# Windowed attention and a gated feed-forward on one core: the raw keys of unit 3 move from the opening's list of steps to the head of the next list, and that list's order changes

## The chip, the cores and the metric

The kernel runs on one core of a Trainium2 chip. The metric is the device time of one execution in microseconds (us); lower is better. The engines are TensorE (PE in the profile, with its weight loads as PEld), VectorE (DVE), ScalarE (ACT), GpSimd (POOL) and SyncE (SP). SP computes nothing; it only issues transfers between DRAM and the chip's memory.

## The reference

Attention over 4 batches, 8 heads, 768 tokens of 64 numbers, then a feed-forward of 512 to 2048 to 512 over the 3072 tokens. Each query sees the keys less than 16 positions away, and 24 more keys and values that are the maximum and the mean of each block of 32 tokens:

```python
k_sum = k.reshape(B, H, nb, block, D).max(axis=3)
v_sum = v.reshape(B, H, nb, block, D).mean(axis=3)
scores_l = scale * np.matmul(q, k.transpose(0, 1, 3, 2))
mask_l = np.abs(pos[:, None] - pos[None, :]) < window
scores_s = scale * np.einsum('bhsd,bhnd->bhsn', q, k_sum) + np.log(block)
...
a = np.exp(scores_all - np.max(scores_all, axis=-1, keepdims=True))
a = a / (np.sum(a, axis=-1, keepdims=True) + 1e-09)
attn = np.matmul(a, np.concatenate([v, v_sum], axis=2))
...
h = x @ w_in
g = np.where(h >= 1, h, np.where(h <= -1, 0.0, (h + 1) ** 2 / 4))
out = g @ w_out
```

All of it is float32.

## The kernel before

**Units.** The tokens are worked in seven units, numbered 0 to 6 in the code: four of 384 tokens and three of 512. "Unit 3" of the title is the third, index 2 in the code, and its steps have a 2 as their first digit; below, units go by the index. Each unit has an attention part, in four pairs of heads (p = 0 to 3), and a feed-forward part, in sixteen blocks of 128 hidden columns (f = 0 to f in hexadecimal). While the feed-forward of unit c runs, the attention of unit c+1 is worked beside it. A float32 product is made of three products of high and low halves, so each weight block is once split into halves: a weight is fetched raw, ACT scales its top words (L237) and its low words (L243), DVE joins them (L250, L255), ACT, DVE or POOL takes the high half (L265) and POOL the rest (L269). This conversion goes on beside units 0 and 1. Units 4 to 6 work with "sets": sums and differences of weight blocks that are kept in DRAM during units 1 to 3 (L636 to L643) and loaded again into the places of the weight blocks by POOL (L580).

**Order.** The whole work is two strings of steps, OPENING and REST. A program walks through each string and issues each step's instructions at once, and each engine runs what it was given strictly in that order; a wait at the head of an engine's queue holds up everything behind it. SP's queue holds all loads and stores but those of the sets, which stand in POOL's queue between its computing. Between the two strings, POOL clears two buffers (L754, L757) that take over memory of the opening.

**Steps.** A step is a letter and hexadecimal digits, mostly unit, pair or block, and part. `r20` is `load_raw_keys(2, 0)`: one DMA of 384 KB (L292). `R20` is `sum_keys`: DVE's maximum over blocks of 32 keys (L352). `C200` is `summary_keys`: POOL copies these maxima into the key tile (L357), beside the window keys that `k20` loads (L303). `s20` multiplies that key tile with the queries of `q20` on PE (L510). `v13` is `load_vals(1, 3)` (L337), `A13` the product that reads those values (o_ps, L449). `y20` loads raw values (L324) and `u20` sums them on DVE (L367). `wf` fetches the last pair of weight blocks to be converted, raw (its two DMAs are `raw<-in_w_out` of L228), `af` is ACT's first pass over it (L237), `bf0`, `bf1` the second (L243), `cf0` to `cf3` the joins on DVE (L250, L255). F is the first product of the feed-forward (`h`, L571), G, H, I, J, O its gate (ACT L664, ACT L668, DVE L672, ACT L677, POOL L682), B the second product (`acc`, L695). T transposes scores (t_ps, L437), N gives their norms (POOL L432), X and L split attention outputs (L460, L465). `{460` loads part 0 of set 6 (L580), and `1460` is the first product that reads it (L594).

**Buffers.** The tiles of the raw keys of units from 2 on, of the raw values of these units and of the windowed values of unit 1 share one tag with two buffers:

```python
def load_raw_keys(c, p):
    k_raw = input_tile(stage, "kraw", [P, S], c, p) if c < 2 else load.tile([P, S], F32, tag="v", name=f"kraw{c}_{p}", bufs=2)
    nc.sync.dma_start(out=k_raw, in_=kT[BEGINS[c][0], p])
...
        v_ts[c, p] = input_tile(load, "v", [P, NB, P], c, p)
```

A DMA into a buffer waits on SP's queue until the last reader of the tile before it is done.

Of the kernel before, what the change touches and what calls it, by code (L numbers as in the profile page):

```python
# [10 lines left out]
I32 = mybir.dt.int32  # L11
U32 = mybir.dt.uint32
# [49 lines left out]
c83 F081 I06 F082 F083 bb1 J07 r20 bb0 F0a0 O07 v11 J06 F0a1 ab q13 F0a2 F0a3 c82 E110 cb0 O06 cb2 cb1 d8 E111 e8 cb3  # L62
D111 G08 B06 N111 H08 db I08 aa S12 W10 M121 ba1 M120 J08 ba0 G0a we f121 ca1 B07 eb F090 F091 ca0 F092 F093 ca3 H0a
ca2 D110 A10 E121 O08 T111 I0a da ac P111 v13 bc1 B08 G09 X10 cc1 F0c0 ea bc0 H09 cc3 F0c1 ad I09 J09 J0a N110 wf cc0
f120 bd0 F0c2 F0b0 O09 cc2 dc F0b1 bd1 cd0 O0a cd2 C13 F0b2 L10 cd1 F0c3 W11 F0b3 B09 T110 E120 D121 cd3 G0c G0b P110
H0b S13 A11 dd H0c B0a ec M130 I0b q21 ed I0c F0d0 D120 k20 ae F0d1 F0e0 F0e1 J0c F0e2 v12 F0d2 M131 J0b f130 be0 r21
f131 ce0 N120 O0c be1 E130 ce2 O0b af D130 F0d3 X11 N121 R20 ce1 F0e3 ce3 B0b L11 E131 G0d H0d I0d B0c bf1 de ee cf1
bf0 G0e H0e T120 I0e cf0 F0f0 cf3 J0d O0d W13 F0f1 cf2 D131 F0f2 J0e df F0f3 T121 q20 G0f F110 H0f F111 W12 P121 N130
P120 N131 T130 A12 X12 I0f T131 P131 L12 F100 J0f P130 B0d O0e R21 ef O0f A13 X13 F112 L13 C200 F101 F102 F113 F103
B0e G11 G10 H10 H11 I10 B0f J10 I11 F120 J11 O10 F121 F122 O11 F123  # L70
# [3 lines left out]
i20 F141 g203 H13 g200 z20 I13 g202 g205 g204 F142 F143 B10 F160 F161 F162 F163 B11 J12 g201 u21 O12 %012 h20 %013 G16  # L74
l201 l200 H16 o01 &10 o02 z21 B12 %001 %000 J13 O13 G14 I16 t202 t20a %014 t205 y22 r22 F150 H14 t209 %002 t207 t200
t206 F151 v20 &61 B13 C210 %015 I14 t208 F170 F171 F152 J16 %016 J14 x200 %017 F153 %003 t204 t20b t203 t201 %004 O14
O16 G15 p20 H15 X20 &05 q22 %005 R22 %006 L20 u22 I15 B14 &01 s21 J15 F172 %007 n211 v21 n210 y23 &02 r23 F173 G17
%101 F180 F181 i21 H17 I17 &51 &11 &03 %100 k22 q23 &04 F182 %102 g213 %103 z22 g212 g211 g215 g214 g210 F183 O15 %104
G18 h21 H18 F190 I18 %105 u23 l210 l211 F191 x210 t216 F192 t215 F193 B15 t219 t21b t214 t210 t212 t211 t217 F1a0 F1a1
J17 F1a2 B16 F1a3 %106 O17 %107 t213 G19 &12 t218 %110 H19 J18 t21a B17 O18 p21 %111 I19 &13 %112 G1a H1a &50 I1a %113  # L80
F1c0 F1c1 X21 C220 L21 F1c2 %114 s22 %115 F1b0 F1b1 %116 n220 n221 %200 i22 J19 %117 %201 g224 F1b2 g223 g225 g220 B18
O19 F1c3 R23 J1a O1a %202 z23 g222 F1b3 g221 %203 h22 G1c %204 H1c G1b I1c v22 &15 k23 l220 l221 H1b %205 B19 I1b %206
F1d0 x220 %207 J1b F1d1 F1d2 F1d3 F1f0 F1f1 O1b t220 t228 t224 t223 G1d F1f2 &14 H1d t222 t225 t221 t22b t227 B1a %210
C230 t229 t22a %211 t226 p22 J1c X22 I1d F1e0 y40 &20 &23 %212 O1c %213 F1e1 L22 F1e2 %214 %215 s23 %301 n231 n230 i23
F1e3 %216 F1f3 G1e B1b %300 H1e g234 g231 v23 &22 g233 J1d I1e %302 F200 %217 g232 %303 &24 k30 g230 O1d %304 g235
F201 G1f H1f %305 x230 F202 h23 B1c %306 J1e &25 &31 l231 l230 I1f %307 O1e t233 t235 t230 t234 F210 %311 q30 %310
F211 &33 B1d J1f B1e t23a t23b t232 t236 t239 t238 t231 O1f t237 p23 X23 u40 %312 %313 L23 B1f F203 C300 U10 G20 s30
F212 %314 H20 %315 o10 %316 n301 F213 G21 I20 J20 n300 H21 F230 F231 F232 i30 g302 g301 I21 %317 r40 k31 v30 &35 J21
g300 U11 g303 g305 g304 O20 F233 F220 G23 F221 F222 F223 O21 G22 H23 B20 o11 h30 l301 l300 x300 C310 H22 I23 %401 I22
# [732 lines left out]
```

## Time and profile before

| what | value |
| --- | --- |
| time, median of 3 runs | 630.86 us (630.76 to 632.21) |
| the profiled execution's own time | 630.26 us |
| its span (first to last instruction) | 628.5 us |
| TensorE's mean granted clock | 0.989 of full speed |
| PE busy | 609.4 us, 97% of the span |
| PEld, DVE, ACT, POOL busy | 85%, 70%, 58%, 63% |
| transfers | 122.56 MB, 195 GB/s on the mean |

Busy times are sums over the span. A share near 100% says that an engine hardly ever rests; where it does rest is read from stretches of the trace (windows), and why, from what released it (waits).

### The profile page before, as it was taken

Reading aid. Unit: us, or ns where it says so; the run is one execution under the profiler, and the core shown is the slowest. Engines: PE = TensorE matmul, PEld = TensorE weight load, DVE = VectorE, ACT = ScalarE, POOL = GpSimd, SP = SyncE. Lnnn points to the kernel's source line nnn. Section 1 sums busy time; section 2 is a strip of 40 time slices with the busy share of each in tenths; the row PEclk is TensorE's granted clock in tenths of the full one; section 3 lists DMA queues with packets and bytes.
Section 4 is the critical chain, followed back from the end, with each engine's and each line's share of the span. In section 5 each row is a group of like instructions: output and inputs, shape, how many; then the busy total and the mean of one; then the engine's idle time right before and its main releaser. Section 6 shows DMA issues by size and latency. Waiting matters only on the chain.

```text
span 628.5 us, 12987 instructions
## 1 busy us (share of the span) xinstructions
PE 609.4 (97%) x4628; PEld 535.5 (85%) x4628; DVE 437.9 (70%) x1012; ACT 365.0 (58%) x977; POOL 393.7 (63%) x450
## 2 busy tenths in 40 slices
PE   8689998999999999999999999999999999999996
PEld 7578887788888888898888988879988898989895
DVE  5879785568887789778676788865777765444342
ACT  2779997456454655565465665537556365553542
POOL 2578997655676677663477865669674568735421
PEclk9879999999999999999999999999999999999998
DMA  8989835476554667355678497767696485676521
GB/s 305 329 238 382 269 100 142 140 275 202 155 157 159 171 169 216 103 141 133 178 216 270 116 304 231 196 197 217 184 302 175 124 269 146 175 225 186 172 64 67
DMA packets 85041, 122.56 MB, mean 195 GB/s; under 512 B 27377, under 2 KB 56305, under 8 KB 84977
## 3 DMA queue, kind: packets, MB, share of 16 engines
q1 hardware_dynamic: 71152, 77.68, 40.6%
q0 software_dynamic: 13824, 44.05, 23.9%
q8 instruction: 37, 0.61, 0.4%
q14 instruction: 28, 0.22, 0.1%
HBM read 100.73 MB, written 20.97 MB: 194 GB/s over the span
## 4 chain that ended last, share of the span: by engine, by line
PE 89%; DVE 3%; DMA 2%; ACT 2%; POOL 2%; issue 2%; SPq 0%; POOLq 0%; ACTq 0%; DVEq 0%
PE acc L695 41%; PE h L571 20%; PE h L594 19%; PE o_ps L559 3%; PE s_ps L510 3%; DMA halves<-sets 1%; PE o_ps L449 1%; PE t_ps L437 1%; DMA first<-in_kT 1%; PE s_ps L403 1%; ACT raw L237 1%; DVE den L416 1%; PE h_idle L650 0%; DVE vs L361 0%; DVE e L410 0%
## 5 line engine op out<-in xcount | busy, mean ns | idle before, releaser
L695 PE MATMUL acc<-halves,ghi 128*128 128x512 f32 x720 | 224.2, 393 | 0.0
L682 POOL TENSOR_TENSOR glo<-t,ghi 128x384 fp32r<-128x384 f32 (+1 forms) x112 | 126.9, 1135 | 108.6 <-ACT ghi L677 98.9
L695 PEld LDWEIGHTS acc<-halves,ghi 128*128 128x128 f32 x720 | 135.5, 188 | 24.5
L571 PE MATMUL h<-x,halves 128*128 128x384 f32 x720 | 140.5, 342 | 3.1 <-POOL halves L269 2.2
L695 PE MATMUL acc<-halves,glo 128*128 128x512 f32 x360 | 143.0, 397 | 0.0
L594 PEld LDWEIGHTS h<-halves,halves 128*128 128x128 f32 x1008 | 132.4, 190 | 9.6 <-issue 1.8
L664 ACT ACTIVATE t<-h,ones_half 128x256 f32<-128x256 f32 (+1 forms) x160 | 80.2, 513 | 101.0 <-DVE h L607 56.7
L594 PE MATMUL h<-halves,halves 128*128 128x256 f32 x1008 | 135.7, 283 | 1.0 <-DMA halves<-sets 1.0
L571 PEld LDWEIGHTS h<-x,halves 128*128 128x128 f32 x720 | 125.1, 188 | 11.1 <-POOL halves L269 3.1
L672 DVE SCALAR_TENSOR_TENSOR t<-h,t 128x256 f32<-128x256 f32 (+1 forms) x160 | 73.6, 472 | 48.4 <-ACT t L668 44.2
L550 DVE STREAM_TRANSPOSE turned_blocks<-e 32x256 f32<-32x256 f32 (+1 forms) x240 | 98.4, 410 | 5.8 <-POOL e L538 1.8
L677 ACT CAST ghi<-t 128x384 fp32r<-128x384 f32 (+1 forms) x112 | 61.9, 556 | 60.3 <-PE acc L695 38.6
L695 PEld LDWEIGHTS acc<-halves,glo 128*128 128x128 f32 x360 | 67.8, 188 | 12.0 <-issue 1.3
L580 POOL DMA_DIRECT2D halves<-sets x96 | 53.1, 556 | 31.8 <-PE h L594 30.6
L668 ACT ACTIVATE t<-t 128x256 f32<-128x256 f32 (+1 forms) x160 | 71.0, 458 | 2.9
L528 ACT ACTIVATE e<-e,den 128x120 f32<-128x120 f32 x144 | 55.0, 383 | 18.6 <-DVE den L524 18.4
L607 DVE TENSOR_TENSOR sums_so_far<-h,sums_so_far 128x256 f32<-128x256 f32 x72 | 29.5, 421 | 34.2 <-PE h L594 29.0
L607 DVE TENSOR_TENSOR h<-h,sums_so_far 128x256 f32<-128x256 f32 x96 | 39.0, 426 | 20.2 <-PE h L594 18.8
L538 POOL TENSOR_TENSOR e<-e,den 128x480 f32<-128x480 f32 (+1 forms) x40 | 35.6, 910 | 26.3 <-DVE den L533 12.1
L269 POOL TENSOR_TENSOR halves<-w,halves 128x1024 fp32r<-128x1024 f32 x15 | 36.1, 2409 | 5.7 <-DMA q<-in_q 4.2
L517 DVE SCALAR_TENSOR_TENSOR e<-s_ps,mask_sb 128x480 f32<-128x480 f32 (+1 forms) x40 | 22.8, 602 | 14.0 <-PE s_ps L510 14.0
L630 POOL TENSOR_TENSOR merged<-merged,high_of_sums 128x512 fp32r<-128x512 f32 x16 | 20.7, 1296 | 17.8 <-ACT high_of_sums L628 17.6
(115 smaller groups left out, 688.7 us busy)
## 6 DMA issues: line engine op xcount, KB each, us to landing
halves<-sets POOLq DMA_DIRECT2D x72, 512.0 KB, 4.8
raw<-in_w_in SPq DMA_DIRECT2D x15, 512.0 KB, 10.3
raw<-in_w_out SPq DMA_DIRECT2D x15, 512.0 KB, 9.6
v<-in_vwin SPq DMA_DIRECT2D x22, 288.0 KB, 4.0
out<-o SPq DMA_DIRECT2D x24, 256.0 KB, 3.8
halves<-sets POOLq DMA_DIRECT2D x24, 256.0 KB, 4.3
kraw<-in_kT SPq DMA_DIRECT2D x13, 384.0 KB, 4.3
vraw<-in_vT SPq DMA_DIRECT2D x13, 384.0 KB, 4.3
```

The costliest lines, as they stand in the source:

```text
L528: nc.scalar.activation(out=e, in_=e, func=AF.Exp, bias=dens[c, p][:, 0, u:u + 1], scale=1.0, accum_out=dens[c, p][:, 1, u:u + 1])
L550: nc.vector.transpose(out=turned_blocks[kb * SB:(kb + 1) * SB, :2 * nt, qb * SB:(qb + 1) * SB], in_=e[qb * SB:(qb + 1) * SB, :, at:at + SB])
L571: nc.tensor.matmul(hs[c, f][:, :w], weight["win", f][:, part, k * P:(k + 1) * P], x, start=(k == 0 and n == 0), stop=(k == NK - 1 and n == 2))
L580: nc.gpsimd.dma_start(out=at[:, 0] if n == 3 else at.rearrange("p h n -> p (h n)"), in_=cols)
L594: nc.tensor.matmul(hs[c, q, n][:, :HALF], weights[:, wp, kk], x[:, xp, kk], start=(kk == 0 and m == 0), stop=(kk == 1 and m == 2))
L607: nc.vector.tensor_tensor(out=of if to is None else so_far[:, to], in0=of, in1=so_far[:, so], op=ALU.add)
L664: nc.scalar.activation(out=t, in_=h, func=AF.Relu, bias=ones_half, scale=0.5)
L668: nc.scalar.square(out=t, in_=t)
L672: nc.vector.scalar_tensor_tensor(out=t, in0=h, scalar=1.0, in1=t, op0=ALU.max, op1=ALU.min)
L677: nc.scalar.copy(out=hi, in_=ts[c, f])
L682: nc.gpsimd.tensor_tensor(out=lo, in0=ts[c, f], in1=hi.bitcast(F32), op=ALU.subtract)
L695: nc.tensor.matmul(acc[c, i], a[:, rows], weight["wout", f][:, part], start=(f == first and n == 0), stop=(f == last and n == 2))
```

## The change

No step is added or taken away. Five steps (`r20`, `r21`, `R20`, `R21`, `C200`) leave OPENING, whose other steps keep their order, and stand near the head of REST. REST is also put in another order in two long parts: from its beginning to about 435 steps in (feed-forward of unit 1, attention of unit 2), and from about 1075 to 1510 (feed-forward of units 3 and 4, attention of unit 5); behind that, a few neighbours change places. The lines of OPENING that lost a step, and the head of REST:

```diff
-c83 F081 I06 F082 F083 bb1 J07 r20 bb0 F0a0 O07 v11 J06 F0a1 ab q13 F0a2 F0a3 c82 E110 cb0 O06 cb2 cb1 d8 E111 e8 cb3
+c83 F081 I06 F082 F083 bb1 J07 bb0 F0a0 O07 v11 J06 F0a1 ab q13 F0a2 F0a3 c82 E110 cb0 O06 cb2 cb1 d8 E111 e8 cb3 D111
...
-H0b S13 A11 dd H0c B0a ec M130 I0b q21 ed I0c F0d0 D120 k20 ae F0d1 F0e0 F0e1 J0c F0e2 v12 F0d2 M131 J0b f130 be0 r21
-f131 ce0 N120 O0c be1 E130 ce2 O0b af D130 F0d3 X11 N121 R20 ce1 F0e3 ce3 B0b L11 E131 G0d H0d I0d B0c bf1 de ee cf1
+S13 A11 dd H0c B0a ec M130 I0b q21 ed I0c F0d0 D120 k20 ae F0d1 F0e0 F0e1 J0c F0e2 v12 F0d2 M131 J0b f130 be0 f131 ce0
+N120 O0c be1 E130 ce2 O0b af D130 F0d3 X11 N121 ce1 F0e3 ce3 B0b L11 E131 G0d H0d I0d B0c bf1 de ee cf1 bf0 G0e H0e
...
-P120 N131 T130 A12 X12 I0f T131 P131 L12 F100 J0f P130 B0d O0e R21 ef O0f A13 X13 F112 L13 C200 F101 F102 F113 F103
+T130 A12 X12 I0f T131 P131 L12 F100 J0f P130 B0d O0e ef O0f A13 X13 F112 L13 F101 F102 F113 F103 B0e G11 G10 H10 H11
...
-y21 U01 U00 U02 F130 y20 &41 &30 k21 &21 &40 o00 %011 s20 F131 &00 u20 G12 %010 F132 F133 n201 H12 I12 n200 G13 F140
...
+F130 U00 &40 r20 r21 k21 &11 R20 C200 U01 y20 o01 F131 G12 U02 F132 R21 H12 s20 I12 o00 y21 n201 F133 F160 v20 G13
```

**SP's queue in the opening.** The first piece shows SP before, from the raw weights of block pair 12 (`raw_943`) on; a name ends in a running number of its buffer, `kraw_0` is `r20`, `v_1` is `v11`, `v_3` is `v13`, `raw_1178` is `wf`, and `q_1` and `k_0` are `q21` and `k20`.

```order
L228 DMA raw_943<-in_w_out 128x1024
L225 DMA raw_943<-in_w_in 128x4x256
L292 DMA kraw_0_984<-in_kT 128x768
L337 DMA v_1_993<-in_vwin 96x768
L319 DMA q_3_1002<-in_q 64x6x64 x2
L228 DMA raw_wout_1074<-in_w_out 128x1024
L225 DMA raw_win_1075<-in_w_in 128x4x256
L337 DMA v_3_1138<-in_vwin 96x768
L228 DMA raw_1178<-in_w_out 128x1024 x2
```

The same place of SP's queue after the change, and on to the place where the raw keys now stand, behind a store of a weight block into the sets (`&40`).

```order
L225 DMA raw_943<-in_w_in 128x4x256
L337 DMA v_1_991<-in_vwin 96x768
L319 DMA q_3_1000<-in_q 64x6x64 x2
L228 DMA raw_wout_1072<-in_w_out 128x1024
L225 DMA raw_win_1073<-in_w_in 128x4x256
L337 DMA v_3_1136<-in_vwin 96x768
L228 DMA raw_1176<-in_w_out 128x1024 x2
L319 DMA q_1_1286<-in_q 64x6x64 x2
L303 DMA k_0_1297<-in_kwin 128x720
L337 DMA v_2_1317<-in_vwin 96x768
L319 DMA q_0_1435<-in_q 64x6x64 x2
L636 DMA sets<-halves_881 128x1024
L292 DMA kraw_0_1602<-in_kT 128x768
```

The load of the raw keys no longer stands ahead of `v11` and takes a buffer of its tag there; what stood behind it moves up one place in the same order, and the two loads of raw keys follow all of the opening's loads.

**POOL's queue where REST begins.** Before, the copy of the key maxima (`C200`, L357) stands ahead of the two gate rows of unit 1 and of the clearing of the two buffers.

```order
L682 TENSOR_TENSOR glo_15_1493<-t_15_1444,ghi_15_1492 128x384
L357 COPY k_0_1299<-ks_0_1356 128x6x24
L682 TENSOR_TENSOR glo_0_1568<-t_0_1553,ghi_0_1567 128x384
L682 TENSOR_TENSOR glo_1_1576<-t_1_1551,ghi_1_1575 128x384
L754 MEMSET turned_blocks 128x1024
L757 MEMSET sums 128x128
L621 TENSOR_TENSOR merged_1_1625<-halves_345 128x256 x2
```

After the change it stands behind them:

```order
L682 TENSOR_TENSOR glo_15_1487<-t_15_1438,ghi_15_1486 128x384
L682 TENSOR_TENSOR glo_0_1559<-t_0_1544,ghi_0_1558 128x384
L682 TENSOR_TENSOR glo_1_1567<-t_1_1542,ghi_1_1566 128x384
L754 MEMSET turned_blocks 128x1024
L757 MEMSET sums 128x128
L357 COPY k_0_1297<-ks_0_1609 128x6x24
L621 TENSOR_TENSOR merged_1_1665<-halves_345 128x256
```

The copy has moved behind four rows of POOL, and on PE `s20`, which reads what it writes, has moved behind two steps of F (`F131`, `F132`).

**POOL's queue at the loads of set 6.** Before: `halves_1020`, `halves_881`, `halves_805` and `halves_941` (DMA rows of L580) are the places that parts 2, 1, 0 and 3 of set 6 go to, `glo_8` is a gate row, and `xraw` and `v_3` are tiles of the attention.

```order
L484 TENSOR_TENSOR xraw_0_4413<-xraw_0_4413 128x512
L379 COPY v_3_4756<-zeros 32x512
L580 DMA halves_1020<-sets 128x1024
L580 DMA halves_881<-sets 128x1024
L580 DMA halves_805<-sets 128x1024
L682 TENSOR_TENSOR glo_8_4970<-t_8_4919,ghi_8_4969 128x512
L580 DMA halves_941<-sets 128x512
```

After, in POOL's order:

```order
L580 DMA halves_941<-sets 128x512
L580 DMA halves_1131<-sets 128x1024
L580 DMA halves_1040<-sets 128x1024
...
L379 COPY v_3_4832<-zeros 32x512
L580 DMA halves_1018<-sets 128x1024
L682 TENSOR_TENSOR glo_8_4974<-t_8_4923,ghi_8_4973 128x512
L580 DMA halves_805<-sets 128x1024
L580 DMA halves_881<-sets 128x1024
```

Part 0 (`halves_805`) has moved ahead of part 1, part 3 (`halves_941`) far ahead of both, and the gate row between part 2 and these.

## Rows read from the trace of the kernel before

**Rows 1.** Windows: us, busy time of each engine (instructions), clock, DMA share, GB/s

```profile
60.00:80.00 20.00, 19.55 (x120) 17.01 (x119) 15.66 (x31) 19.97 (x41) 18.96 (x15) 1.00 0.82 266
80.00:100.00 20.00, 19.98 (x162) 17.41 (x161) 15.98 (x34) 18.51 (x41) 18.51 (x15) 1.00 0.38 111
100.00:120.00 20.00, 16.97 (x127) 14.35 (x127) 11.62 (x24) 11.21 (x28) 14.27 (x16) 1.00 0.40 109
...
400.00:420.00 20.00, 19.04 (x144) 16.61 (x144) 16.40 (x43) 12.25 (x38) 13.27 (x18) 1.00 0.86 240
```

**Rows 2.** PE's timeline: start us, us, instruction, [idle before <-what ended it]

```profile
106.37 0.49 PE L437 MATMUL t_ps<-ident_sb,e 128*120 128x128 f32 x3
108.44 2.34 PE L571 MATMUL h<-x,halves_win 128*128 128x384 f32 x12 [1.58 <-DVE t L672]
111.66 0.55 PE L437 MATMUL t_ps<-ident_sb,e 128*120 128x128 f32 x3 [0.88 <-DVE w L255]
...
113.83 0.54 PE L437 MATMUL t_ps<-ident_sb,e 128*120 128x128 f32 x3 [0.57 <-POOL e L432]
114.30 0.92 PE L449 MATMUL o_ps<-pt,v 120*64 120x64 f32 x24
...
128.65 0.85 PE L510 MATMUL s_ps<-k,q 64*64 64x120 f32 x24
```

**Rows 3.** ACT's timeline

```profile
79.61 1.14 ACT L237 ACTIVATE raw<-raw 128x1024 f32<-128x1024 f32 x1
...
103.96 1.15 ACT L237 ACTIVATE raw<-raw 128x1024 f32<-128x1024 f32 x1 [2.93 <-DMA raw<-in_w_out]
```

**Rows 4.** SP's timeline around the raw keys

```profile
69.35 1.09 SPq L292 DMA_DIRECT2D kraw<-in_kT  x1
85.00 0.33 SPq L337 DMA_DIRECT2D v<-in_vwin  x1
...
96.05 0.33 SPq L337 DMA_DIRECT2D v<-in_vwin  x1
96.83 1.06 SPq L228 DMA_DIRECT2D raw<-in_w_out  x2
```

**Rows 5.** SP's waits, 60 to 130 us: in all, times, longest

```profile
SPq L337 <- PE o_ps L449: 22.6, 2, 14.5
```

**Rows 6.** The page, DMA issues: line, count, KB each, median us to landing

```profile
halves<-sets POOLq DMA_DIRECT2D x72, 512.0 KB, 4.8
...
raw<-in_w_out SPq DMA_DIRECT2D x15, 512.0 KB, 9.6
```

**Rows 7.** DVE's timeline

```profile
101.35 0.92 DVE L352 TENSOR_REDUCE ks<-kraw 128x24 f32<-128x768 f32 x1
...
107.74 0.56 DVE L672 SCALAR_TENSOR_TENSOR t<-h,t 128x384 f32<-128x384 f32 x1 [1.68 <-ACT t L668]
...
110.93 1.28 DVE L255 SCALAR_TENSOR_TENSOR w<-raw,c 128x512 int32<-128x512 int32 x2
...
123.31 1.02 DVE L672 SCALAR_TENSOR_TENSOR t<-h,t 128x384 f32<-128x384 f32 x2 [3.04 <-ACT t L668]
```

**Rows 8.** POOL's timeline

```profile
105.55 1.29 POOL L269 TENSOR_TENSOR halves_win<-w,halves_win 128x512 fp32r<-128x512 f32 x1
...
112.99 1.54 POOL L432 TENSOR_TENSOR e<-e,den 128x360 f32<-128x360 f32 x2
...
128.64 0.20 POOL L757 MEMSET sums<- 128x128 f32 x1
...
404.97 1.05 POOL L580 DMA_DIRECT2D halves<-sets  x2 [2.05 <-PE h L594]
```

**Rows 9.** The chain that ended last, 400 to 416 us: start us, us, what

```profile
405.49 8.45 DMA halves<-sets
```

**Rows 10.** DMA issues, 60 to 85 us: count, KB each, median us to landing

```profile
raw<-in_w_in SPq DMA_DIRECT2D x2, 512.0 KB, 8.2
kraw<-in_kT SPq DMA_DIRECT2D x1, 384.0 KB, 8.1
```

More of the change, by code (lines that the diff above doesn't have):

```diff
@@ new lines @@
+G08 B06 N111 H08 db I08 aa S12 W10 M121 ba1 M120 J08 ba0 G0a we f121 ca1 B07 eb F090 F091 ca0 F092 F093 ca3 H0a ca2
+D110 A10 E121 O08 T111 I0a da ac P111 v13 bc1 B08 G09 X10 cc1 F0c0 ea bc0 H09 cc3 F0c1 ad I09 J09 J0a N110 wf cc0 f120
+bd0 F0c2 F0b0 O09 cc2 dc F0b1 bd1 cd0 O0a cd2 C13 F0b2 L10 cd1 F0c3 W11 F0b3 B09 T110 E120 D121 cd3 G0c G0b P110 H0b
+S13 A11 dd H0c B0a ec M130 I0b q21 ed I0c F0d0 D120 k20 ae F0d1 F0e0 F0e1 J0c F0e2 v12 F0d2 M131 J0b f130 be0 f131 ce0
+N120 O0c be1 E130 ce2 O0b af D130 F0d3 X11 N121 ce1 F0e3 ce3 B0b L11 E131 G0d H0d I0d B0c bf1 de ee cf1 bf0 G0e H0e
@@ L71 @@
+T120 I0e cf0 F0f0 cf3 J0d O0d W13 F0f1 cf2 D131 F0f2 J0e df F0f3 T121 q20 G0f F110 H0f F111 W12 P121 N130 P120 N131
+T130 A12 X12 I0f T131 P131 L12 F100 J0f P130 B0d O0e ef O0f A13 X13 F112 L13 F101 F102 F113 F103 B0e G11 G10 H10 H11
+I10 B0f J10 I11 F120 J11 O10 F121 F122 O11 F123
 """
 REST = """
[L73 to L74 removed]
@@ L75 @@
[L75 to L89, printed above, removed]
@@ new lines @@
+9430 J45 G441 G440 (421 x511 {442 O45 t519 t514 (420 H441 1432 H440 (423 t516 t512 t515 t513 t517 t510 (422 I440 t518
+(453 I441 x520 u53 {440 s52 n521 (450 o32 n520 J44 {443 i52 9431 g527 g520 g521 1436 (452 1434 g525 g524 g522 g523
+g526 z52 p51 1433 9432 X51 9434 1435 O44 {441 {452 x521 9437 9436 G461 G470 1431 h52 9435 H461 G471 H470 (440 l520
+H471 (451 (442 l521 I461 9433 (443 I470 (441 I471 J47 G460 1443 1440 9440 k53 O47 v53 1444 t522 t529 t521 t520 1442
+t52a {463 (470 H460 {450 {451 t525 C530 t524 t526 I460 J46 t527 (472 9441 1441 (471 t528 t52b O46 ^50 {453 1446 9442
@@ new lines @@
+O4a p53 X53 9465 (4b2 1470 <50 G4d1 s60 (4b1 H4d1 (4b3 n600 I4d1 x600 {471 ^51 1465 ^52 >50 n601 9466 1466 (4a2 1461
+9467 {501 {503 G4d0 H4d0 I4d0 9463 {502 (4a0 G4c1 J4d G4c0 9470 i60 1471 {500 <51 (4a3 O4d H4c0 1472 (4a1 H4c1 g601
+g603 I4c0 9473 (4d3 I4c1 (4d2 >51 9471 1474 1473 {510 ^53 9472 9474 (4d0 9475 1475 1476 J4c g605 <52 g600 g604 g607
+g606 <54 O4c G4f1 9476 g602 h60 H4f1 I4f1 G4f0 9477 >52 G4e0 H4f0 G4e1 I4f0 >54 <53 H4e1 <55 l600 l601 >53 (4c2 (4d1
+(4c3 1500 (4c0 1504 I4e1 H4e0 9500 <56 >55 J4f 1502 (4c1 I4e0 9501 1501 1503 t601 9502 O4f {511 J4e t604 1505 1510
@@ new lines @@
+1603 G600 H600 9604 9602 (5e0 (5e2 (5e3 I600 >66 9605 <65 1606 >65 G611 H611 (5e1 9607 I611 U51 G601 U50 H601 1605
+9606 I601 G610 1614 1610 1612 H610 9610 {623 {622 {621 I610 o51 o50 {620 9611 1613 9612 9614 1611 J60 J61 O61 1616
+1615 O60 9617 9615 G631 9613 9616 (611 H631 U52 I631 G630 G621 H630 U53 G620 (613 (603 (601 (612 (602 (610 H621 H620
+{632 {630 I630 I621 J63 I620 1620 (600 9620 J62 O63 1622 1624 O62 1621 (632 (633 (630 9621 9622 9623 1623 1626 (631
+G640 1625 (622 (620 (623 9624 {631 9625 9627 9626 G651 G641 H641 H651 G650 H650 H640 (621 I650 I651 I641 1630 1634
@@ new lines @@
+1660 J6b O68 {673 9660 G6a1 {670 (682 O6b {672 H6a1 (683 G6a0 H6a0 (681 I6a0 I6a1 (680 1664 (6b2 (6b0 1662 (6b1 1663
+9661 9664 J6a 9662 9665 G6d1 (6b3 O6a H6d1 {671 I6d1 (6a3 1665 1666 (6a1 1661 (6a0 9667 9666 9663 G6d0 (6a2 H6d0 I6d0
+G6c1 1670 1674 J6d H6c1 9670 G6c0 I6c1 1672 9671 9672 H6c0 O6d 1673 9674 I6c0 (6d1 1675 9675 (6d3 1676 J6c G6f1 1671
+(6d2 (6d0 O6c 9676 G6f0 H6f1 H6f0 I6f1 9677 9673 G6e1 I6f0 G6e0 J6f H6e0 (6c2 H6e1 O6f (6c0 (6c3 (6c1 (6f0 I6e1 I6e0
+J6e O6e (6f1 (6f3 (6f2 (6e2 (6e0 (6e1 (6e3 U62 U60 U61 U63 o62 o63 o61 o60
```

169 lines of the change are left out of this document (80 added, 89 removed).

## The prediction

> **What bounds the kernel now.** I read the windows first, then PE's timeline where they show a gap, then the timelines of the engines that PE waited for, and last SP's queue. PE is busy for 97% of the span, so the question is only where it is not. In the windows [rows 1] the reader is to compare the first busy column with 20: 19.98 from 80 to 100 us, 16.97 from 100 to 120, 19.04 from 400 to 420. The windows between, and those behind up to 600, show 19.9 or more. Time that is won ahead of such windows is won at the end, since PE's order there doesn't depend on when it starts; so two gaps count, 20 - 16.97 = 3.03 us and 20 - 19.04 = 0.96 us.
>
> PE's timeline [rows 2] splits the first one: 1.58 us before the last half-block of F0f, released by the gate's DVE row of L672; 0.88 us before the next transposes, released by a weight join (L255), which holds the same kind of accumulator; 0.57 us before the third, released by POOL's norms (L432). Together 3.03 us, the whole gap. Three engines are named, but one lateness stands behind them. ACT stood idle for 2.93 us up to 103.96 [rows 3], waiting for the raw weights of the last pair (`wf`). All that ACT does behind it, gate and conversion, is late, and DVE and POOL with it: 107.74, 110.93 and 112.99 [rows 7, 8].
>
> Why were these weights late? SP issued them at 96.83 [rows 4], and they took some 7 us. They stood behind `v13`, and `v13` behind `v11`. SP's waits [rows 5] say that two loads of L337 waited 22.6 us in all for the products that read earlier values, the longest 14.5 us. The timeline shows them [rows 4]: `kraw` (r20) goes out at 69.35 and takes one of the two buffers; `v11` must wait for the other until 85.00, when `A10` has read `v10`; `v13` must wait for `v11` to be read, until 96.05. So raw keys that REST needs sit in a buffer for 32 us (69.35 to their maximum on DVE at 101.35 [rows 7]) and leave one buffer for three values.
>
> **The opening after the change.** `r20` is gone from SP's queue there. `v11` finds a free buffer and goes out at about 69.4; the queries and the weights of block pair 13 follow it as soon as a transfer before them lands. `v13` is now the one that waits for `A10`, so it goes out at 85.0, where `v11` went (PE was full up to there, so `A10` keeps its time). `wf` follows 0.8 us later (96.83 - 96.05 [rows 4]), at 85.8 and 86.4. With the median landing of this load, 9.6 us [rows 6], the second lands at 96.0; ACT is ready for it at 103.96 - 2.93 = 101.03 [rows 3]. That leaves 5 us to spare, so ACT's wait of 2.93 us goes.
>
> What is late next, gap by gap, is found by shifting each row by 2.93 us:
> - Gate row L672 ends at 107.74 + 0.56 - 2.93 = 105.37. PE reaches the place at 108.44 - 1.58 = 106.86. POOL's lower half of the same weights ended at 105.55 + 1.29 = 106.84 [rows 8], and it gets earlier by the 0.92 us of `R20`, which leaves DVE ahead of the join that it waits for [rows 7]: 105.9. The 1.58 us are all won.
> - The first of the two joins ended about 111.57 (half of 1.28 us behind 110.93), so 108.64. PE gets there at 111.66 - 2.46 = 109.20. The 0.88 us are won.
> - The first norm ends at 112.99 + 0.77 - 2.93 = 110.83. PE gets there at 113.83 - 3.03 = 110.80. This one is at its edge; I leave 0.2 us of it, and at most all 0.57 us.
>
> So the opening gives 3.03 - 0.2 = 2.8 us; 1.58 if only the first gap closes.
>
> As to how much a window lost, the Trainium skill (Perfetto Trace Analysis, Identifying the Most-Contended Engine) holds matmul busy time to be a bad measure and the busy share of weight loads a good one. By that the stretch from 100 to 120 us did 14.35 us of loads where its neighbour did 17.41 [rows 1], an estimate of 20 x (1 - 14.35 / 17.41) = 3.5 us lost instead of 3.03. I stay with 3.03, which is the sum of named waits; the two stretches hold different mixes of product lengths.
>
> **The head of REST, where the five steps now stand.** Their work is the same and moves: two loads, 0.92 us twice on DVE, one short copy on POOL. `r20` waits for `A12`, which ends at 114.30 + 0.92 - 2.8 = 112.4 [rows 2]; `r21` for `A13`. The one slow landing that the trace shows took 8.1 us [rows 10], so the keys are there at 120.5. `R20` stands on DVE behind the gate rows that ended at 123.31 + 1.02 = 124.33 [rows 7], now 121.5; before them DVE was idle for 3.04 us, so both sums are hidden. `C200` now stands behind POOL's two clearings, which ended at 128.84 [rows 8], and ends some 0.3 us later, 129.1 less 2.8. `s20` on PE, which reads it, started at 128.65 [rows 2]; two steps of F of 3 products each, 2.34 / 12 = 0.195 us a product, now stand ahead of it, so it comes at 129.8 less 2.8. That is 0.7 us of cover; without it, each late microsecond costs one. I put the edit at 0.
>
> **The loads of set 6.** The gap at 413 us is a wait for one load. The chain [rows 9] shows it issued at 405.49 and landing after 8.45 us, where the median of its kind is 4.8 [rows 6]. It was the second of a pair that POOL issued at 404.97 [rows 8], so one load of 512 KB more stood ahead of it. The new order puts it ahead of that one, and part 3 well ahead of both. At the window's 240 GB/s [rows 1] 512 KB take 2.1 us, more than the wait of 0.96 us, but POOL still waits for the reader of the place, and a gate row stands ahead. I take 0.7 us, with 0 and 0.96 as bounds.
>
> **The rest of the reordering** (units 1 to 4) lies in windows where PE never waits, so it can win nothing; its possible loss is a rival.
>
> **The sum.** 630.26 - 2.8 - 0.7 = 626.8 for the profiled execution. The median stands 0.6 above it (630.86), so 627.4. Ends of this case: 630.86 - 3.03 - 0.96 = 626.9 and 630.86 - 1.58 = 629.3.
>
> **Rivals.**
> 1. *Another engine takes over.* Only the first gap closes, since joins and norms were the true limit of the other two, and the load of set 6 stays as late: 629.3. For it: the third gap has no margin in my own working. Against it: each row behind 103.96 follows ACT. 0.12.
> 2. *The change doesn't do what it says.* `v13` still waits for `A11`, because the buffers come round in another order, and `wf` goes out at 96.8: 630.86 - 0.7 = 630.2. 0.04.
> 3. *The transfers collide.* Without the long wait, `v11`, two query loads and the weights of pair 13 (288 + 192 + 1024 KB) follow at once on those of pair 12, while 60 to 80 us moves 266 GB/s already [rows 1]: 1504 less 384 KB of raw keys is 4.3 us of transfer. If all of that fell on the loads ahead, the last of them, out before 69.35 and there 8.2 us later by its median [rows 10], at 77.5, would land at 81.8, where ACT takes it at 79.61 [rows 3]: 2.2 us late, of which ACT's idle 1.5 us in that stretch (20 - 18.51 [rows 1]) takes most. At worst PE loses 2.2, and the time is 629.6; if ACT's slack counts, 628.1. The Trainium skill (DMA: Bandwidth & Descriptors, Issuing engines are not separate DMA queues) says that all transfers run on the same 16 engines and interleave, which speaks for this rival. Against it: these loads stand behind the others on one queue. 0.06, half of it within 0.3%.
> 4. *The raw keys come too late* (the other side). `R20` heads DVE's queue, and behind it stand the copies of unit 0's results, the gate of unit 1 and the scores. `C200` can be late by 0.7 us only, so the keys must have landed by 129.8 - 2.8 - 0.3 - 0.92 = 125.8, 13.4 us after 112.4. Beyond that each microsecond costs one on PE; the kernel is slower than before by over 0.3% (1.9 us, about what a measurement of it can tell from no change) if they land 3.5 + 1.9 = 5.4 us later still, 18.8 us after their issue. Stores to the sets run beside them there. Two such waits, for `R20` and `R21`, could also share it. Time at 6.5 us: 633.9. With whatever the new order of units 1 to 4 brings of late loads of the kind at 405.49, 0.08.
>
> **Chances and range.** My forecast 0.70. Faster: 0.70 and half of rival 3, 0.73. Same: rivals 1, 2 and half of 3, 0.19. Slower: 0.08. The range goes from 626.0 (0.9 below the better end, since runs of one kernel differed by 0.6 from the profiled one and a load's landing can be better than its median) to 630.2, rival 2; above it lies rival 4 and below it about 0.05.
>
> **What would show it.** SP issues `v11` near 69.4, `v13` near 85 and `wf` near 86; ACT has no wait for `raw` near 101; the window of 100 to 120 us has PE at 19.7 or more; `s20` has no wait for POOL's L357; the wait for `halves<-sets` is under 0.3 us. The prediction is wrong if `wf` goes out near 96 still, if PE waits for L432 or L255 as long as before, or if new waits stand between 120 and 270 or 335 and 412 us.

## The result

| | before | after |
| --- | --- | --- |
| median | 630.81 us (629.08 to 632.21, 6 runs) | 624.89 us (623.58 to 627.80, 6 runs) |
| ratio | | 0.9914, 95% interval 0.9888 to 0.9941 |
| the profiled execution, its span, its mean clock | 630.26, 628.5, 0.989 | 627.80, 626.0, 0.988 |

The change makes the kernel 0.9% faster, by 5.9 us between the medians; 3.4 had been forecast, with 626.0 us as the lower end of the range. The direction and the places were right and the size was not. Run again beside 29 runs of the kernel before, the changed kernel took 624.78 us against 630.20: 5.4 us, ratio 0.9918 (0.9897 to 0.9938).

The profiled execution of after is the slowest of its six. It lost time ahead of the change: the first product of `A10` stood at 84.00 us before and at 86.14 here, 2.1 us later, though both kernels have the same instructions up to about 69 us. The windows of after (us, busy time of PE, PEld, DVE, ACT, POOL with instructions, clock, DMA share, GB/s) show where:

```profile
20.00:40.00 20.00, 15.07 (x143) 12.92 (x144) 15.43 (x38) 15.51 (x53) 11.23 (x12) 0.69 1.02 299
40.00:60.00 20.00, 19.15 (x154) 16.41 (x154) 16.79 (x33) 18.04 (x39) 16.08 (x12) 0.96 0.91 306
80.00:100.00 20.00, 19.97 (x178) 16.79 (x177) 16.43 (x37) 18.91 (x40) 18.47 (x15) 1.00 0.42 124
100.00:120.00 20.00, 19.52 (x144) 17.34 (x143) 11.16 (x23) 12.85 (x31) 16.41 (x17) 1.00 0.22 68
...
400.00:420.00 20.00, 20.00 (x177) 17.85 (x177) 16.33 (x41) 10.57 (x34) 12.21 (x16) 1.00 0.77 201
```

The granted clock (last but two) was 0.69 and 0.96 in the first two rows, where the kernel before had 0.74 and 1.00. Such luck in the first 60 us is left out of what follows by counting from `A10` on. These are the rows of `A10` on PE, before and after:

```profile
84.00 0.92 PE L449 MATMUL o_ps<-pt,v 120*64 120x64 f32 x24
```

```profile
86.14 0.92 PE L449 MATMUL o_ps<-pt,v 120*64 120x64 f32 x24
```

In the fourth row of the windows PE is busy for 19.52 us where it was 16.97, in the last for 20.00 where it was 19.04 [rows 1]: the two gaps that the prediction named are nearly gone. (As a sign it had named 19.7 or more for the fourth row; what is missing is the third part of the first gap.)

SP's timeline of after, to be set beside [rows 4]; the times are shifted by those 2.1 us:

```profile
71.24 0.99 SPq L337 DMA_DIRECT2D v<-in_vwin  x1
...
87.16 0.33 SPq L337 DMA_DIRECT2D v<-in_vwin  x1
87.53 0.90 SPq L228 DMA_DIRECT2D raw<-in_w_out  x2
...
114.47 4.22 SPq L292 DMA_DIRECT2D kraw<-in_kT  x2
```

`v11` waits no more; `v13` is released by `A10` at 87.16 (85.0 in the old count, as forecast), and the last raw weights follow at 87.53. ACT's timeline shows the first pass over them without any wait, at 101.0 in the old count, where 101.03 was worked out:

```profile
103.01 0.20 ACT L421 ACTIVATION_READ_ACCUMULATOR e<-e,den 128x1 f32 x1
103.11 1.14 ACT L237 ACTIVATE raw<-raw 128x1024 f32<-128x1024 f32 x1
```

PE's timeline, beside [rows 2]: two of the three gaps are gone, of the third 0.48 us are left.

```profile
108.55 0.49 PE L437 MATMUL t_ps<-ident_sb,e 128*120 128x128 f32 x3
108.80 2.34 PE L571 MATMUL h<-x,halves_win 128*128 128x384 f32 x12
110.97 0.49 PE L437 MATMUL t_ps<-ident_sb,e 128*120 128x128 f32 x3
111.22 1.30 PE L571 MATMUL h<-x,halves 128*128 128x384 f32 x6
113.00 0.54 PE L437 MATMUL t_ps<-ident_sb,e 128*120 128x128 f32 x3 [0.48 <-POOL e L432]
...
115.22 0.39 PE L695 MATMUL acc<-halves_wout,glo 128*128 128x512 f32 x1
```

**Where the time came from.** Two marks divide the run: the first product with `halves_wout`, and the scores of 32 products near 284 us, which lie behind the first reordered part. These are PE's rows of before:

```profile
116.06 0.39 PE L695 MATMUL acc<-halves_wout,glo 128*128 128x512 f32 x1
...
284.86 1.05 PE L510 MATMUL s_ps<-k,q 64*64 64x120 f32 x32
```

and this is the second of after:

```profile
283.14 1.05 PE L510 MATMUL s_ps<-k,q 64*64 64x120 f32 x32
```

- From `A10` to the first mark: 116.06 - 84.00 = 32.06 before, 115.22 - 86.14 = 29.08 after, 2.98 us won.
- From there to the second: 168.80 before, 167.92 after, 0.88 us won.
- From there to PE's last product: 622.73 - 284.86 = 337.87 before, 620.26 - 283.14 = 337.12 after, 0.75 us won. The last product is the second of these two of before,

```profile
622.51 0.61 PE L695 MATMUL acc<-halves,ghi 128*128 128x512 f32 x2
```

and the second of these two of after:

```profile
620.03 0.61 PE L695 MATMUL acc<-halves,ghi 128*128 128x512 f32 x2
```

That is 4.6 us between these two executions, against 3.5 forecast. The rest of the 5.4 to 5.9 between medians was what the experiments had to find.

### The profile page after: what moved, and what is told of

Same layout as the page of the kernel before. It is cut to its first block, busy times and chain, and to the rows that moved or that the text cites. A ratio compares the mean times of both kernels' runs of the same rounds, so it can differ in the third digit from the quotient of the medians.

```text
span 626.0 us, 12988 instructions
## 1 busy us (share of the span) xinstructions
PE 610.1 (97%) x4628; PEld 537.4 (86%) x4628; DVE 440.5 (70%) x1012; ACT 365.3 (58%) x977; POOL 394.3 (63%) x450
## 4 chain that ended last, share of the span: by engine, by line
PE 91%; ACT 3%; DMA 3%; POOL 1%; issue 1%; SPq 0%; DVE 0%; ACTq 0%; POOLq 0%; DVEq 0%
PE acc L695 42%; PE h L571 21%; PE h L594 19%; PE o_ps L559 3%; PE s_ps L510 3%; DMA raw<-in_w_in 2%; PE o_ps L449 1%; PE t_ps L437 1%; DMA first<-in_kT 1%; PE s_ps L403 1%; ACT raw L237 1%; ACT c L243 1%; ACT e L421 1%; ACT t L664 0%; POOL halves L269 0%
## 5 line engine op out<-in xcount | busy, mean ns | idle before, releaser
L580 POOL DMA_DIRECT2D halves<-sets x96 | 53.3, 557 | 35.0 <-PE h L594 32.3
```

The source lines that it names most:

```text
L580: nc.gpsimd.dma_start(out=at[:, 0] if n == 3 else at.rearrange("p h n -> p (h n)"), in_=cols)
```

## The experiments

Theory A after the two traces: three pieces (opening, first and second part of REST), and the granted clock of the first 60 us for the rest. Theory B: a single piece holds what is missing. The kernel before ran beside each group, 17 to 29 times, with medians of 629.83 to 630.20 us. The ratios and their intervals are reckoned over all the runs and not from the two medians; they differ from the medians' quotient by up to 0.001. In the rows of the first four runs below, lines are smaller by one.

**The changed kernel again** (no edit).

> The changed kernel once more, beside the kernel before on the same chip, to see the time of each run beside its granted clock. Theory A (three pieces plus the clock): the trace of the change showed 2.9 us won in the opening, 0.9 us between 120 and 270 us and 0.8 to 1.1 us near 345 to 415 us, 4.6 us in all; the rest of the 5.9 us between the medians is the granted clock of the first 60 us, which differs from run to run in any kernel. Then this time, with both kernels' clocks drawn anew, the medians differ by about 4.6 us (3.8 to 5.4), and the time of the runs of one kernel falls by about 0.5 us for each 0.001 of clock. Theory B (all of it is the change's): the medians differ by 5.9 us again and the changed kernel's clock is higher each time.

Measured: 624.78 us (624.65 to 625.69) against 630.20 (627.90 to 633.08), 5.4 us. That is the upper edge of what theory A allows. The mean clocks are 0.9925 and 0.9915; at the 0.5 us for 0.001 that theory A reckoned with, that could be 0.5 us of it. The scatter says more: at mean clocks of 0.992 to 0.994 the kernel before took 627.94 to 632.38 us (35 runs of all groups), the changed kernel at 0.993 took 624.32 to 625.34 (8 runs of both comparisons). Something in the kernel before varies that doesn't vary here. The trace of this run also shows that the clock made `A10` late in the first one: with the granted clock of before in the first 60 us (0.74 and 1.00) `A10` starts at 84.01 us, at 84.00 before, so the loads that now go out earlier cost nothing up to there.

**The opening alone.**

```diff
-y21 U01 U00 U02 F130 y20 &41 &30 k21 &21 &40 o00 %011 s20 F131 &00 u20 G12 %010 F132 F133 n201 H12 I12 n200 G13 F140
+r20 R20 C200 r21 R21 y21 U01 U00 U02 F130 y20 &41 &30 k21 &21 &40 o00 %011 s20 F131 &00 u20 G12 %010 F132 F133 n201
```

with OPENING as in the change.

> The five steps leave the opening and stand at the very front of REST, whose order stays that of before. Theory A: the opening's 2.9 us come alone: the window of 100 to 120 us has PE at about 19.5 as in the changed kernel, the first pair of late raw weights is issued near 88 and ACT doesn't wait for it; time 2.4 to 2.9 us less than before (the front of REST may take back some tenths, since SP's loads of raw values now wait behind the maxima). The wait for the set's part near 413 us stays at about 1 us. Rival (the first gap was only moved): the gaps come back at the head of REST, where s20 waits for the key maxima, and the time is within 1 us of before.

Measured: 628.25 us, 2.0 us less (0.9975, 0.9961 to 0.9990), a little under what was expected. From `A10` to the first mark it took 29.11 us, all that the changed kernel has; but the old front of REST took some of it back. PE's timeline there:

```profile
125.51 0.85 PE L509 MATMUL s_ps<-k,q 64*64 64x120 f32 x24 [0.42 <-POOL k L356]
126.29 1.86 PE L570 MATMUL h<-x,halves 128*128 128x384 f32 x9
128.86 2.38 PE L570 MATMUL h<-x,halves 128*128 128x384 f32 x12 [0.70 <-DVE t L671]
```

Here `s20` stands two steps of F earlier than in the change, and it waits for the copy of the key maxima behind POOL's clearings. The keys themselves were in time; behind `s20` PE waits for a gate row that stands on DVE behind sums of raw values, whose load landed late. So the path is not the one that rival 4 of the prediction described (keys that land too late), but the price is of its kind: gaps of 1.1 us, and 170.52 us from the first mark to the second, 1.7 more than before. In the change, the reordered front of REST avoids it: the copy ends at 127.96 + 0.30 = 128.26 and `s20` starts at 128.86, 0.6 us of cover where 0.7 had been worked out. Those rows of POOL and of PE after:

```profile
127.96 0.30 POOL L357 COPY k<-ks 128x144 f32<-128x144 f32 x1
```

```profile
128.86 0.85 PE L510 MATMUL s_ps<-k,q 64*64 64x120 f32 x24
```

There was another wait of 1.0 us near 552 us for a copy of results on DVE, which the run of all but the second part shows too (1.07 us at 550.74) and no other trace does. It wasn't followed up.

**The first part of REST alone.** OPENING as before, with the five steps in it; the first 430 steps of REST, which then lack them, in the new order:

```diff
-y21 U01 U00 U02 F130 y20 &41 &30 k21 &21 &40 o00 %011 s20 F131 &00 u20 G12 %010 F132 F133 n201 H12 I12 n200 G13 F140
+F130 U00 &40 k21 &11 U01 y20 o01 F131 G12 U02 F132 H12 s20 I12 o00 y21 n201 F133 F160 v20 G13
...
```

> The opening as before, with r20 in it; only the first 430 steps of REST take the order of the change. Theory A: the gap of 3 us at 100 to 120 us stays as it was, and between 120 and 270 us 0.9 us are won in waits and switches of 0.1 to 0.2 us each that no window shows: 0.6 to 1.0 us less than before. Theory B: this part holds what the sum lacked, 2 us or more. The prediction had put it at nothing.

Measured: 629.49 us, 0.7 us less (0.9990, 0.9971 to 1.0009); in the times alone that can't be told from nothing. The trace supports it: from the first mark to the last product 505.18 us, 1.5 less than before, of which 0.5 is a shorter wait near 412 us; from the first mark to the second 167.86, 0.94 less.

**The second part of REST alone.** OPENING and the rest as before, steps 1075 to 1509 in the new order:

```diff
-{411 O3b G3d t433 t430 F3e3 H3d x430 t438 B3b {412 {413 I3d
+t433 t438 t430 {411 F3e3 O3b X42 {412 G3d B3b x430 H3d G3e
...
```

> The opening as before; only the steps 1075 to 1509 of REST take the order of the change (loads of sets 4 to 6, attention of unit 5, products of unit 4). Theory A: the wait for the part of set 6 near 413 us is gone (1.0 us), and a new one of about 0.3 us stands near 346: 0.7 to 1.1 us less than before. Theory B: 2 us or more. Rival: within 0.3 us, because what is won at 413 is lost around it.

Measured: 629.36 us, 0.8 us less (0.9993, 0.9975 to 1.0010), in size as expected and again less than the runs can tell from nothing. Its trace speaks for the rival: the wait near 413 us is gone, but 0.46 us of waiting for another part of a set stands near 465 us, and from the second mark to the last product it took 337.77 us, 0.10 less than before.

Both of these runs have the old opening, and in both the low clock appears behind the gap. Windows of the second (columns as above):

```profile
104.00:108.00 4.00, 2.58 (x13) 1.65 (x11) 0.56 (x1) 3.28 (x10) 2.34 (x2) 1.00 0.19 54
108.00:112.00 4.00, 2.85 (x9) 2.88 (x10) 2.60 (x5) 3.34 (x7) 1.01 (x1) 0.64 0.00 0
```

PE was busy for 2.58 of 4 us, and then the granted clock is 0.64 over the next 4, part of it at the lower of its two levels, 1.2 instead of 2.4 GHz. So I formed a theory for the missing microsecond: in the old opening the clock falls behind the gap in some executions, though it hadn't in the profiled one.

**The gap filled.** The transposes ahead of the first gap are done five times over, so that PE would work through it:

```diff
-        for t in range(NT):
+        for t in [*range(NT)] * (5 if (c, p, j) == (1, 2, 0) else 1):
```

> The kernel before, but the three transposes of unit 1's third pair that stand ahead of the first gap are done five times over instead of once, so that PE works through most of the 1.6 to 1.9 us in which it waited. Nothing becomes available earlier. Theory A (behind the gap the granted clock falls in some executions, which adds to the gap): the window of 100 to 120 us keeps a clock of 1.00, the twelve products behind the gap take 2.3 us and not 3.8, the three gaps add up to no more than before; time 0.3 to 1.0 us less than before, since the fall is avoided where it would come. Rival (the low clock in the two runs with the old opening has nothing to do with the gap): the clock falls to 0.9 there again, and the time is the same as before or up to 0.3 us longer.

Measured: 629.85 us, the same as before (1.0003, 0.9983 to 1.0023). PE still paused, 1.75 us ahead of these transposes and 0.47 behind them. The clock stayed at 1.00, but the stretch from `A10` to the first mark was 34.19 us, longer than in any trace with the old opening unfilled. The clock is not what makes it long. What does is in ACT's timelines of these executions, the wait for the last raw weights: the first part of REST alone,

```profile
104.01 1.13 ACT L236 ACTIVATE raw<-raw 128x1024 f32<-128x1024 f32 x1 [3.42 <-DMA raw<-in_w_out]
```

the second part alone,

```profile
104.69 1.14 ACT L236 ACTIVATE raw<-raw 128x1024 f32<-128x1024 f32 x1 [4.15 <-DMA raw<-in_w_out]
```

the gap filled,

```profile
105.16 1.13 ACT L237 ACTIVATE raw<-raw 128x1024 f32<-128x1024 f32 x1 [5.12 <-DMA raw<-in_w_out]
```

and the two loads swapped (below).

```profile
102.33 1.14 ACT L237 ACTIVATE raw<-raw 128x1024 f32<-128x1024 f32 x1 [2.84 <-DMA raw<-in_w_out]
```

Set beside the stretch from `A10` to the first mark:

| old opening | ACT's wait | `A10`, first mark | the stretch |
| --- | --- | --- | --- |
| loads swapped | 2.84 | 82.44, 114.41 | 31.97 |
| before | 2.93 | 84.00, 116.06 | 32.06 |
| first part of REST | 3.42 | 83.55, 116.11 | 32.56 |
| second part of REST | 4.15 | 83.56, 116.76 | 33.20 |
| gap filled | 5.12 | 83.04, 117.23 | 34.19 |

The stretch follows ACT's wait nearly microsecond for microsecond, with the clock low in the third and fourth row and full in the others. The wait depends on when the second load lands, and that varied; with the new place of `r20` the same stretch took 29.08, 29.04, 29.11 and 29.05 us in four traces, since there the load lands 8.5 to 9.3 us ahead of its use. The low clock seems to have cost little: the slower products ran in time that the second and third gap would have taken (in the second part's run PE has no gap at all at the second set of transposes).

**One step moved.** Of the whole change only `r20`, and only as far as the fetch of the last raw weights:

```diff
-c83 F081 I06 F082 F083 bb1 J07 r20 bb0 F0a0 O07 v11 J06
+c83 F081 I06 F082 F083 bb1 J07 bb0 F0a0 O07 v11 J06
...
-J09 J0a N110 wf cc0
+J09 J0a N110 wf r20 cc0
```

> The kernel before with one step moved: r20 stands right behind the fetch of the last raw weights instead of ahead of v11; its maximum on DVE, the copy on POOL and all of REST stay. Theory A (the place of one load in SP's queue is the whole cause of the opening's gaps): the last raw weights are issued near 86, ACT doesn't wait for them, PE's gaps of 100 to 120 us shrink to about 0.5 us, and 3.0 to 3.6 us are won against before, about 2 us more than with the five steps at the front of the old REST, since the maxima of the keys are ready early here. Rival (the maximum on DVE, L352, has its part in it): over 1 us of gaps stays, and the time is 2 us or less below before.

Measured: 627.09 us, 2.9 us less (0.9954, 0.9936 to 0.9973, so 1.7 to 4.0 us). SP's timeline:

```profile
84.68 0.33 SPq L337 DMA_DIRECT2D v<-in_vwin  x1
85.05 0.91 SPq L228 DMA_DIRECT2D raw<-in_w_out  x2
96.13 0.33 SPq L292 DMA_DIRECT2D kraw<-in_kT  x1
```

The weights go out 11 us earlier than before (85.05 against 96.83 [rows 4]) and the stretch takes 29.05 us, though the maximum on DVE and the copy on POOL are still in the opening. The place of this one load in SP's queue is the cause of the opening's gaps; that four other steps left with it is worth nothing there.

**The two loads swapped.**

```diff
-(461 g531 g532 I490 {461 {460 1453
+(461 g531 g532 I490 {460 {461 1453
```

> The kernel before with two neighbours of REST swapped: the load of part 0 of set 6 stands ahead of that of part 1. Theory A (the wait near 413 us is that of a load behind another of its kind): that wait, 1.0 us in the trace before and 0.5 to 0.9 in other looks at the same order, goes to nothing or nearly, nothing else changes; time 0.4 to 1.0 us less. Rival (what is short is the transfer rate, so the other part is late then): the wait moves to another product within 10 us and the time is the same.

Measured: 629.12 us, 0.8 us less (0.9991, 0.9976 to 1.0006); the times alone can't tell that from nothing, but the trace can: from the second mark to the last product 337.03 us, 0.84 less than before. The chain of work that ended last runs over PE alone there, without the load that stood in it [rows 9]:

```profile
409.00 2.75 PE acc L695 x12
411.75 0.71 PE h L594 x6
```

The wait is gone and no other part became late. In the change this load goes out at 402.48 or 403.64, and PE has no wait for a set behind 400 us in that trace; in the trace of the changed kernel run again one of 0.46 us stands near 460 us.

**All but the second part.** The new opening and the new first 435 steps of REST, old from there on.

> The changed opening and the changed first 435 steps of REST, with the rest of REST as before. Theory A (the pieces add up): opening 3.0 to 3.5 us and 0.9 us between 120 and 270 us, without the price that the old front of REST had for the late maxima (waits of 0.6 and 0.9 us near 125 to 128 us in the run of the opening alone): 4.0 to 4.6 us less than before, and the wait near 413 us stays. Rival (the second part has most of what the sum of pieces lacks): 3 us or less below before.

Measured: 625.64 us, 4.3 us less (0.9942, 0.9921 to 0.9963), and the wait near 410 us is there (0.7 us), beside the 1.07 us at 550.74 named above. The pieces add up as far as the interval (2.3 to 5.0 us) can tell.

**The weights later.** The other way round, in the kernel before:

```diff
-J09 J0a N110 wf cc0
+J09 J0a N110 cc0
...
-ed I0c F0d0 D120 k20 ae F0d1
+ed I0c F0d0 D120 k20 wf ae F0d1
```

> The kernel before with the fetch of the last raw weights moved the other way: behind k20 and its wait, some 3 us later in SP's queue (near 100 instead of 96.8). Theory A (ACT's wait for these weights is the cause, microsecond for microsecond, and the clock falls behind a long gap): ACT waits 5 to 8 us instead of 2.9 to 4.2, PE's stretch up to the last weights' second product gets 2 to 4 us longer, the granted clock falls to half for some microseconds behind the gap, and the time is 2.5 to 5 us above before. Rival (PE's gaps have a second cause that hides behind this one, so that the weights are not what ends them): time within 1 us of before.

Measured: 631.12 us, 1.3 us more (1.0023, 1.0005 to 1.0041): the sign as expected, the size a miss. The profiled execution, its slowest at 634.98, has the expected shape. ACT's row, and the window behind PE's gap:

```profile
107.51 1.10 ACT L237 ACTIVATE raw<-raw 128x1024 f32<-128x1024 f32 x1 [5.68 <-DMA raw<-in_w_out]
```

```profile
112.00:116.00 4.00, 4.00 (x13) 3.90 (x14) 3.00 (x7) 2.40 (x6) 2.20 (x3) 0.50 0.00 0
```

The stretch took 35.70 us, 3.64 more than before for 2.75 us more of waiting; the 0.9 us beyond (3.64 - 2.75) I put down to the clock at 0.50, the lower level. The other eleven runs (629.83 to 633.64) have no trace. Five of the twelve had a mean clock of 0.988 or less and took 632.47 us or more, seven had more and took 631.41 us or less: it looks as if the clock fell in some of them only, and the median is of those where it didn't. That the loads came sooner in these is a guess.

**Three attempts on the last 0.5 us.** In the changed kernel, the copies of mean values go ahead of a gate row on POOL:

```diff
-T120 I0e cf0 F0f0 cf3 J0d O0d W13 F0f1
+T120 I0e cf0 F0f0 cf3 J0d W13 W12 O0d F0f1
...
-G0f F110 H0f F111 W12 P121
+G0f F110 H0f F111 P121
```

> The changed kernel with one more move: the two copies of mean values into the value tiles (POOL, L391), which stand ahead of the norms that the last gap of the opening waits for, go ahead of the gate row before them, where POOL is idle for 1.2 us. Theory A (that gap of 0.5 to 0.6 us is POOL's own order): the gap at L437 behind POOL's L432 goes to under 0.2 us, 0.3 to 0.5 us less than the changed kernel. Rival (DVE's sums end last there anyway): the gap stays at 0.4 us or more and the time is the same.

Only `r20` moved, with the REST of the change:

> r20 alone moved (behind the fetch of the last raw weights), the other four steps stay in the opening; REST in the order of the change. Theory A: the opening's gain hangs on this one step, so the time is that of the changed kernel, within 0.6 us. Rival (the late place of the other four steps has its own worth, by room on DVE and POOL in the opening): 1 us or more above the changed kernel.

Both edits together:

> As the run before (one step moved, REST of the change), with the two copies of mean values ahead of the gate row on POOL as well. Theory A: 0.3 to 0.5 us below the changed kernel, the fastest of all. Rival: the copy of the key maxima, which stands in the opening here, takes the room on POOL, and nothing is won.

Measured: 624.74, 625.04 and 624.68 us; 0.9913, 0.9914 and 0.9915 of before, each with an interval of about 0.002 to either side. The gap itself did go in the first of them, as POOL's and PE's rows show:

```profile
106.33 1.59 POOL L391 COPY v<-mean 24x768 f32<-24x768 f32 x2
108.00 1.02 POOL L682 TENSOR_TENSOR glo<-t,ghi 128x384 fp32r<-128x384 f32 x1
108.98 1.61 POOL L432 TENSOR_TENSOR e<-e,den 128x360 f32<-128x360 f32 x2
```

```profile
110.42 0.49 PE L437 MATMUL t_ps<-ident_sb,e 128*120 128x128 f32 x3
```

and the stretch took 28.66 us instead of 29.08, but 0.4 us can't be told apart in the times. None of the three beats the changed kernel measurably; the second says again that one moved step carries the opening's part.

## Why the prediction was half right

**The opening, forecast 2.8 us: the mechanism right, the size short.** The steps held: `v11` waits no more, `v13` goes out where `A10` ends, the last weights follow 0.4 us later, ACT has them in time, and two of three gaps close (2.98 us won in the stretch, 2.55 of it in the gaps; the third keeps 0.48 us where 0.2 had been left; the run with the copies of mean values moved shows that it was POOL's own order). The step that failed is the bound: "Together 3.03 us, the whole gap", taken from one execution, whose ACT had waited 2.93 us. Over the five traces with the old opening that wait was 3.69 us on the mean, 0.76 more, so the opening is worth 2.98 + 0.76 = 3.7 us on an estimate from these rows. The prediction used the median of the landing, 9.6 us [rows 6], to ask whether the new place is early enough, and didn't ask how much the old place cost when the landing was worse. It also took the wait for the end of the range: "Ends of this case: 630.86 - 3.03 - 0.96". The times don't show that the opening is worth more than forecast: with `r20` moved alone they give 2.9 us, 1.7 to 4.0, which holds the 2.8 as well as the 3.7.

**The first part of REST, forecast nothing: wrong, 0.9 us.** "It can win nothing" rested on windows with PE busy for 19.95 us or more of 20. Between the two marks the windows are as full in the change, and the same products end 0.88 us earlier. These are the two stretches (columns as above), before and after, with 1217 products each:

```profile
116.06:284.86 168.80, 168.74 (x1217) 146.41 (x1217) 129.25 (x305) 92.43 (x249) 104.30 (x122) 1.00 0.58 176
```

```profile
115.22:283.14 167.92, 167.92 (x1217) 146.53 (x1216) 130.69 (x306) 92.45 (x249) 104.81 (x122) 1.00 0.59 175
```

A full window says that PE had no visible pause, not that its products came at their closest: all but 0.06 us of what was won lies inside rows that the timeline shows as one. The second row here, of before, is such a one; its 20 products take nearly as long as the 24 of the first, also of before:

```profile
98.06 4.35 PE L571 MATMUL h<-x,halves 128*128 128x384 f32 x24
...
202.25 4.08 PE L571 MATMUL h<-x,halves 128*128 128x384 f32 x20
```

The busy share of the weight loads, taken over such a stretch of equal work, does tell the two apart: 146.41 of 168.80 us, 86.7%, and 146.53 of 167.92, 87.3%. (From two windows of unequal work, the prediction's estimate by this share was 3.5 us for the first gap, where 2.98 were won.) Which edit wins which delay wasn't tried.

**The loads of set 6, forecast 0.7 us: right.** The swap alone wins the wait (1.0 us in the trace before), and its trace and its median give 0.8 us. (A slip in that paragraph, 2.1 us for 512 KB at 240 GB/s where it is 2.2, changes nothing.)

**The head of REST, forecast nothing: right, and for the reason given.** The opening alone showed what the missing cover costs (0.42 us of waiting for the copy, 1.1 with the gap behind it) and the changed kernel the cover (0.6 us).

**The sum.** 3.7 + 0.9 + 0.8 = 5.4 us, the 5.4 of the second comparison. That the two agree to a tenth is luck, since the interval there is 3.9 to 6.5 us; the 5.9 of the first holds what six runs of each leave open. The traces of these runs, each counted from its own `A10`, bear the sum out; the first row rests on the same five traces as the 3.7. The table has the mean in us, and in brackets the range and the number of traces:

| stretch | old order | new order | won |
| --- | --- | --- | --- |
| `A10` to the first mark | 32.80 (31.97 to 34.19, 5) | 29.06 (29.01 to 29.11, 6) | 3.7 |
| first to second mark | 168.88 (168.72 to 169.07, 6) | 167.88 (167.84 to 167.92, 7) | 1.0 |
| second mark to the last product | 337.70 (337.32 to 338.18, 5) | 337.00 (336.55 to 337.77, 6) | 0.7 |

Left out are traces whose own edit lies in the stretch (the weights later and the copies moved in the first row, the loads swapped in the third; the filled gap is kept, since its stretch is in line with ACT's wait), and those with the waits of the opening alone near 125 to 129 us (second row) and near 551 us (third row, two traces). In the first two rows the ranges don't come near each other; in the third they overlap. A share of the clock of the first 60 us (theory A) isn't needed for the sum but isn't ruled out, up to the 0.5 us named with the first experiment; that the clock behind the gap does fell with the fifth. The sum draws on a mean of five traces, and no experiment held the landing fixed in the old place.

**The rivals.** That another engine takes over didn't come: joins and norms followed ACT. The collision of transfers didn't either: ACT's passes between 74 and 100 us have no wait for raw weights in the trace of after, though 1.1 MB more went out in a row, and at equal clocks `A10` starts at the same time (84.01 and 84.00). By the rule of the Trainium skill (DMA: Bandwidth & Descriptors, Issuing engines are not separate DMA queues) all transfers run on the same 16 engines and interleave. That would fit the load that varied, the second of the last raw weights, which took 6.1 to 8.1 us in five traces of the old opening; no run here shows it, since what shared the engines with that load wasn't taken apart.

## What to carry to other kernels

A load that is asked for long before its use isn't free when it takes one of few buffers and stands at the head of an in-order queue: follow what waits behind it, two and three loads on. A wait for a transfer that one trace shows is one draw; look at several traces, since removing it is worth the mean of the wait, 3.69 us in five traces here where one had shown 2.93. And a window in which the engine is always busy is no proof that reordering can't win: measure between the same two marks in both.

## What the runs showed of the hardware

- The second raw load took 6.1, 6.4, 7.0, 7.7 and 8.1 us to land from the same place of the queue, and ACT's wait and the stretch up to the first mark followed.
- Behind a gap of PE the granted clock fell to half in three traces (PE busy 2.58 of 4 us, then 0.64 over 4 us; 0.50 for a whole 4 us behind the longest gap). These are the traces where ACT waited 3.42, 4.15 and 5.68 us. In the two where it waited 2.84 and 2.93 the clock stayed at 1.00, and so it did where the gap was partly filled, though PE paused 1.75 us there too. Where it fell behind the usual gap it cost next to nothing as far as the stretch shows (32.56 and 33.20 us, in line with the waits); the products behind it would have waited anyway.
- The clock of 20 to 60 us differs from run to run ahead of any edit: 0.69 and 0.96, 0.74 and 1.00; this moved `A10` by 2.1 us, and with 0.74 and 1.00 in both kernels `A10` differs by 0.01 us.
